# A spectral filter and a dense layer over one LayerNorm, on one core: W1 loaded in rows, the first two tiles worked with the contraction outermost, two more tiles turned by DMA

## The chip, the core and the metric

The kernel runs on one core of a Trainium2 chip. The core has five engines that run their own instruction lists: TensorE (PE: matmul, with its weight loads shown as PEld), VectorE (DVE), ScalarE (ACT), GpSimd (POOL) and SyncE (SP, which here only issues DMAs). They meet through semaphores. Data lies in DRAM, in SBUF (128 partitions) and in PSUM (eight banks of 512 f32 columns for 128 partitions, which TensorE writes). The metric is the device time of one execution in microseconds; the profile's span is the part of it that the hardware profiler shows.

## What is computed

```python
xn = _layernorm(x, axis=-1)                       # x: (1, 2048, 640) bf16
# A: spectral filter over both axes
X = rfft2(xn.astype(float32)) * (w_r + 1j * w_i)   # 2048 x 321
a = irfft2(X, s=(2048, 640)).astype(bfloat16)
# B: dense layer
h = gelu(xn @ w1 + b1)                            # w1: 640 x 1536, tanh form of gelu
b = h @ w2 + b2                                   # w2: 1536 x 640
return x + a + b
```

## The kernel before, in words

The 2,048 tokens are 16 tiles of 128; token 16p + c lies in partition p of tile c. Each tile goes through these steps:

- **x load** (`load_x`, L585): tiles 0 and 1 alone (160 KB each), the rest in pairs (320 KB).
- **LayerNorm** on VectorE: two `bn_stats` (L662) of 320 columns, one `bn_aggr` (L664), then rstd on GpSimd (L666), then the norm itself, one `tensor_scalar` of 640 columns (L684) into the tile `T`.
- **Turning.** The first layer contracts over the 640 columns, so the normed tile is transposed into `xnT`, as five blocks of 128 x 128 (the index j). Tiles 0 to 5 are turned by TensorE (L703, five transposes a tile into a PSUM tile `tps`), and copied to `xnT` by VectorE (L558) or ScalarE (L557). The tiles in `BYDMA` (L449), 6 to 15, are turned by a DMA that SP issues (L691).
- **First layer** (L735 to L753): W1 is held as five rows of 1,536 columns, one for each j. `BLOCKS` (L446) says which tiles are worked together: tile 0 alone, tile 1 alone, then pairs, then fours. For each block and each of 12 column groups fc, five matmuls over j, in two steps of three and two, fill one PSUM bank `hps`, and ScalarE puts the gelu of it into `gT` (L751). A matmul is 128 columns wide for a block of one tile, 256 for two, 512 for four.
- **Stage A** on the same normed tiles: VectorE folds a pair of tiles (L713, L717), TensorE multiplies by `gtab` (ten matmuls of 128 columns a pair), the result is copied into `XV`. The later stages of the filter (etab, mtab, the product with W at L818, ntab, getab, htab) follow from about 45 us on.
- **Second layer** (`second`, L904): from `gT` and W2, closed by the filter's last product, added to x + b2 on VectorE and stored.

W1 comes in four transfers (`W1P`, L447, `load_w1`, L592), cut by column groups: fc 0 to 2, 3 to 6, 7 to 9, 10 and 11. Each carries all five rows j, as pieces of 768, 1,024, 768 and 512 bytes, and a group fc needs the one transfer that holds its columns.

**Order.** Every operation gets a number as it is made (`K.op`), and `ORDER` (L159) writes out by hand, for each engine, the list of numbers in which it issues them; an engine never passes an instruction that waits. Waits are worked out from what each operation reads and writes. SP's list is the order of its one DMA queue. The tables `ROW_NS` and `LAG` stand in a model of time in `schedule`, which with a written order only decides which PSUM banks and buffers are taken.

SP's list begins 8 (x tile 0), 12 (x tile 1), 13, 14 (W1 pieces 0, 1), 15 (x tiles 2 and 3), 16, 17 (W1 pieces 2, 3), 19 (x 4 and 5), 18 (gtab), and so on; 165 and 167 are the turns of tiles 6 and 7, behind ten more loads.

Of the kernel before, what the change touches and what calls it, by code (L numbers as in the profile page):

```python
# [9 lines left out]
ACT = mybir.ActivationFunctionType  # L10
# [3 lines left out]
D = 640  # L14
F = 1536
# [83 lines left out]
def mm_us(n):  # L99
    return max(n / 2400.0 + 0.0027, 0.0265)  # L100
# [24 lines left out]
class Pool:  # L125
# [34 lines left out]
    "sp": """8 12 13 14 15 16 17 19 18 20 25 29 21 26 48 24 30 34 42 165 167 28 49 44 178 180 191 193 47 41 27 36  # L160
38 33 32 40 39 206 204 220 218 46 43 35 31 50 37 45 52 525 522 523 524 546 549 548 547 51 572 573 570 571 596 594
595 597 623 650 659 640 614 695 676 686 767 758 712 732 722 783 749 792 799 806""",
    "pe": """7 53 116 114 121 119 235 236 238 239 232 271 233 274 272 268 269 275 283 284 250 251 280 281 247 248 244 245 277 286 278 241
# [8 lines left out]
777 710 778 730 720 747 779 780 786 793 787 781 794 795 788 796 789 790 797 800 801 802 803 804""",  # L172
    "act": """11 9 10 117 54 122 237 240 234 273 270 276 285 252 282 249 246 279 288 243 294 255 291 261 136 264 300 330 309 297 306 131
# [3 lines left out]
578 579 651 590 593 468 615 750 759 480 687 465 474 477 599 775 784 626 471 483 662 697 735 734 769 770""",  # L177
    "dve": """0 55 56 59 57 60 61 113 118 115 120 123 124 127 125 63 64 68 65 67 69 134 126 137 128 139 140 141 145 144 75 74
# [15 lines left out]
class Ring:  # L194
# [4 lines left out]
    def issue_end(self, t, us, n):  # L199
        end = t + us  # L200
        while True:
# [770 lines left out]
```

## Time and profile before

| | us |
|---|---|
| median of 3 runs (149.04 to 149.48) | 149.30 |
| the profiled execution | 149.13 |
| its span | 147.1 |
| busy in it: VectorE | 109.9 |
| ScalarE | 85.8 |
| GpSimd | 23.0 |

Times in the profile's rows are microseconds from the span's start. A row of a timeline reads: start, length, engine, line of the kernel, operation, what it writes and reads, shapes, and how many in a row (x24); a row of several starts with the first and ends with the last, and rows can overlap, since instructions are pipelined. In brackets stands how long the engine idled before it and what it waited for. `ps` is PSUM, `T` the normed tiles, `W` in a matmul of `xnT,W` is W1. All matmuls but the transposes have one line, L546, and are told apart by their operands. TensorE's clock was granted in full in every slice of the span.

### The profile page before, as it was taken

The page shows a single profiled execution, that of the slowest core. Times are in us where ns is not written, and L with a number is a line of the kernel's source. Part 1 is how long each engine was busy: PE and PEld are TensorE (multiplying, and loading weights), DVE is VectorE, ACT ScalarE, POOL GpSimd, SP SyncE. Part 2 cuts the span into 40 slices and gives each one's busy share as a digit, 9 for nine tenths or more (in the row PEclk, how much of TensorE's full clock was granted, in tenths as well). Part 3 has the DMA queues.
Part 4 walks back from the last instruction along what each step waited for, and adds up shares of the span by engine and source line. Part 5 has one row for each costly group of instructions (what it writes and reads, how often), then busy time and mean ns, then how long its engine had stood idle before and what let it go on. Part 6 is the DMA issues. An engine that isn't in the chain of part 4 may idle for free.

```text
span 147.1 us, 4193 instructions
## 1 busy us (share of the span) xinstructions
PE 142.4 (97%) x1766; PEld 92.2 (63%) x1766; DVE 109.9 (75%) x231; ACT 85.8 (58%) x160; POOL 23.0 (16%) x38
## 2 busy tenths in 40 slices
PE   7799999999999999999999999999999999999993
PEld 7599999898465455456544555544447665656572
DVE  1888999999864458799687991893207899987883
ACT  3298898998899999934346637523935730312000
POOL 1302250402200007810000010200076300000000
PEclk9999999999999999999999999999999999999999
DMA  4999999995998974997706651952639950422324
GB/s 106 322 346 395 382 233 132 166 119 128 324 176 154 244 167 92 228 261 138 96 0 113 104 117 32 137 103 49 128 61 231 238 147 1 152 75 89 134 96 134
DMA packets 31546, 23.35 MB, mean 159 GB/s; under 512 B 19240, under 2 KB 28200, under 8 KB 31400
## 3 DMA queue, kind: packets, MB, share of 16 engines
q1 hardware_dynamic: 28992, 17.48, 51.6%
q0 software_dynamic: 2368, 5.57, 17.2%
q8 instruction: 14, 0.23, 0.6%
q10 hardware_dynamic: 168, 0.04, 0.1%
q14 instruction: 4, 0.03, 0.1%
HBM read 13.58 MB, written 2.62 MB: 110 GB/s over the span
## 4 chain that ended last, share of the span: by engine, by line
PE 94%; DMA 2%; DVE 1%; POOL 1%; issue 1%
PE ps L546 93%; DMA X<-in_A_x_dram 2%; PE ps L703 1%; POOL rstd L666 1%; DVE stats L662 1%; DVE T L684 0%; DVE W L929 0%; DVE mv L664 0%
## 5 line engine op out<-in xcount | busy, mean ns | idle before, releaser
L546 PE MATMUL ps<-xnT,W 128*128 128x256 bf16 (+2 forms) x420 | 58.7, 288 | 0.1
L546 PE MATMUL ps<-W,gT 128*128 128x512 bf16 (+2 forms) x396 | 58.5, 295 | 0.0
L546 PEld LDWEIGHTS ps<-W,gT 128*128 128x128 bf16 x396 | 30.1, 98 | 23.1 <-issue 1.5
L546 PEld LDWEIGHTS ps<-xnT,W 128*128 128x128 bf16 x420 | 34.5, 98 | 15.8 <-issue 1.9
L751 ACT ACTIVATE gT<-ps,b1col 128x256 bf16<-128x256 f32 (+2 forms) x84 | 38.4, 509 | 9.8 <-PE ps L546 9.2
L557 ACT ACTIVATE Wf<-ps 128x960 bf16<-128x960 f32 (+1 forms) x8 | 6.7, 869 | 16.9 <-PE ps L546 16.9
L662 DVE BATCH_NORM_STATS2 stats<-X 128x6 f32<-128x320 bf16 x32 | 14.2, 474 | 2.6 <-DMA X<-in_A_x_dram 2.6
L818 DVE TENSOR_TENSOR T<-Y,Wf 128x1288 bf16<-128x1288 bf16 x16 | 12.3, 826 | 1.5 <-DMA Wf<-in_A_w_i_dram 0.9
L914 POOL DMA_DIRECT2D X<-in_A_x_dram x8 | 7.1, 1091 | 38.1 <-DMA XV<-U 21.3
L666 POOL TENSOR_TENSOR rstd<-mv,mhalf 128x2 f32<-128x2 f32 (+1 forms) x10 | 7.1, 706 | 30.6 <-DVE mv L664 30.5
L557 ACT ACTIVATE Xb<-ps 128x960 bf16<-128x960 f32 (+1 forms) x8 | 8.7, 1124 | 5.0 <-PE ps L546 4.9
L914 POOL DMA_DIRECT2D xnT<-in_A_x_dram x8 | 7.1, 1249 | 23.1 <-DMA XV<-U 14.7
L557 ACT ACTIVATE XV<-ps 128x1280 bf16<-128x1280 f32 (+3 forms) x12 | 9.9, 858 | 0.9 <-PE ps L546 0.9
L557 ACT ACTIVATE U<-ps 128x512 bf16<-128x512 f32 (+1 forms) x12 | 4.6, 434 | 8.0 <-PE ps L546 7.9
L558 DVE CAST Y<-ps 128x644 bf16<-128x644 f32 x7 | 5.8, 827 | 4.2 <-PE ps L546 4.2
L717 DVE TENSOR_TENSOR T<-T 128x512 bf16<-128x512 bf16 (+1 forms) x32 | 8.8, 311 | 0.1
L920 DVE TENSOR_TENSOR X<-ps,X 128x640 f32<-128x640 f32 x8 | 6.5, 818 | 3.0 <-PE ps L546 3.0
L558 DVE CAST Wf<-ps 128x960 bf16<-128x960 f32 (+1 forms) x4 | 4.3, 1074 | 5.7 <-PE ps L546 5.7
L929 DVE TENSOR_TENSOR W<-ps,xnT 128x640 bf16<-128x640 f32 (+2 forms) x10 | 6.7, 686 | 2.2 <-PE ps L546 2.2
L684 DVE TENSOR_SCALAR T<-X,mv,rstd 128x640 bf16<-128x640 bf16 x16 | 6.8, 443 | 1.3 <-POOL rstd L666 1.1
L557 ACT ACTIVATE Y<-ps 128x644 bf16<-128x644 f32 x9 | 6.3, 706 | 2.6 <-PE ps L546 2.5
L546 PE MATMUL ps<-getab,XV 32*128 32x160 bf16 (+1 forms) x128 | 7.5, 241 | 0.0
(49 smaller groups left out, 134.2 us busy)
## 6 DMA issues: line engine op xcount, KB each, us to landing
W<-in_B_w_dram SPq DMA_DIRECT2D x6, 480.0 KB, 7.4
X<-in_A_x_dram POOLq DMA_DIRECT2D x8, 320.0 KB, 5.2
xnT<-in_A_x_dram POOLq DMA_DIRECT2D x8, 320.0 KB, 5.4
out_dram<-W SPq DMA_DIRECT2D x15, 160.0 KB, 1.8
X<-in_A_x_dram SPq DMA_DIRECT2D x7, 320.0 KB, 9.2
Wf<-in_A_w_i_dram SPq DMA_DIRECT2D x6, 160.5 KB, 4.4
Wf<-in_A_w_r_dram SPq DMA_DIRECT2D x6, 160.5 KB, 5.6
W<-in_B_w_dram SPq DMA_DIRECT2D x1, 640.0 KB, 6.3
```

The lines of the kernel that those rows point to most:

```text
L546: ins = e.matmul(o_, lhsT=lw, rhs=rh, start=st, stop=sp_, skip_group_check=True)
L557: return e.activation(dst(), src(), ACT.Copy, scale=scale)
L558: return e.tensor_copy(dst(), src())
L662: st_op[c] = K.op([("dve", 0.393)], pr, lambda e, _, c=c, h=h: e.bn_stats(stats[:, c, 6 * h:6 * h + 6], view(X, c * D + H2 * h, [[1, H2]]) ...
L666: K.op([("pool", 0.65)], 500, lambda e, _, a=a, b=b: e.tensor_tensor(out=rstd[:, a:b], in0=mv[:, a:b, 1], in1=mhalf[:, a:b], op=ALU.pow), ...
L684: o = K.op([("dve", 0.356)], pr, lambda e, _, c=c, n=n, xnv=xnv: e.tensor_scalar(out=xnv(n, 0, [[1, D]]), in0=view(X, c * D, [[1, D]]), sc ...
L717: ring_ops.append(K.op([("dve", dve_us(4 * w, 2))], pr, lambda e, _, op=op, x1v=x1v, xfv=xfv, o_=o_, o0=o0, o1=o1, w=w: e.tensor_tensor(ou ...
L751: K.op([("act", act_us(128 * nt, 1))], pr + PRIO["gelu"] + GP[bi], lambda e, _, c0=c0, nt=nt, fc=fc, hps=hps: e.activation(gT[:, fc, 128 * ...
L818: filt_ops.append(K.op([("dve", dve_us(4 * KP, 2))], pr, lambda e, _, k=k, Y=Y, TB=TB, pair=pair: e.tensor_tensor(out=view(TT, TB.slot * 8 ...
L914: xo_ops[c] = K.op([("pool", 0.9)], 51 - c / 20, lambda e, _, c=c, xov=xov: e.dma_start(xov(0, D), xv[:, c, :], accum_op=ALU.add), reads=[ ...
L920: kept_ops.append(K.op([("dve", dve_us(D))], 30, lambda e, _, kps=kps, xov=xov: e.tensor_tensor(out=xov(0, D), in0=psb(kps.slot, [[1, D]]) ...
L929: K.op([("dve", dve_us(w))], 95, lambda e, _, os_=os_, fps=fps, o0=o0, w=w, xov=xov, base=base: e.tensor_tensor(out=view(W1, OST + os_.slo ...
```

## The change

Four things are changed in the program, and the order of all engines is written anew.

1. **W1 in five transfers**, one for each row j: 128 partitions of 3,072 bytes, 384 KB each (`load_w1`). A matmul of the first layer in tiles 2 to 15 now names all five as read, one of the first block only its own row j.
2. **Tiles 0 and 1 in one block.** `BLOCKS` begins with (0, 2). In this block two column groups share one PSUM bank (256 columns each), so that six banks hold all twelve, and the operation is one pair of groups and one j. For j < `LONE` = 2 there is one operation for each of the two tiles (two matmuls of 128 columns), for j = 2 to 4 one for both (two matmuls of 256). Of one pair only the first operation (j = 0, tile 0) has to stand ahead of the others, which the lists may put in any order. The gelu works on both tiles, 256 columns.
3. **Tiles 0 and 1 turned in other parts.** Blocks j = 0, 1 are transposed together and copied by ScalarE, j = 2 to 4 together and copied by VectorE (before: 0 to 2 VectorE, 3 and 4 ScalarE). Tile 0's norm is cut in two, 256 columns and 384, and its first two transposes wait for the first only. The later blocks have buffer names of their own (`B_xnL`), so that a matmul waits for its part alone.
4. **Tiles 4 and 5 turned by DMA** (`BYDMA` from 4), issued by SP.

The numbers in the new lists: SP's 8 and 12 are x tiles 0 and 1, 13, 14, 15, 17, 18 the rows of W1, 16 x tiles 2 and 3, 20, 21, 22 the pairs from 4, 6 and 8, 19 gtab, 26, 30, 27 the pairs from 10, 14 and 12, 25 the first part of W2, 154 and 152 the turns of tiles 5 and 4, 165 and 167 those of 6 and 7. On TensorE 7 is the warm-up, 54 turns b1, 116 and 118 turn tile 0 (j = 0, 1 and j = 2 to 4), 121 and 123 tile 1, 137 and 140 tiles 2 and 3; 232 to 285 are the first block, nine numbers for each pair of groups (for the first: 232 and 233 are j = 0 of tiles 0 and 1, 234 and 235 j = 1, 236, 237, 238 j = 2, 3, 4, and 239 and 240 the two gelus); 286 to 321 are tiles 2 and 3, three numbers for each group, 322 to 357 tiles 4 and 5; 131 and 132, 148 and 149, 161 and 162 are stage A of the first three pairs. On VectorE 56 and 57 are tile 0's statistics and 58 its aggregate, 60 to 62 the same for tile 1, 114 and 115 the two parts of tile 0's norm, 120 tile 1's, 119 and 124 copies of turned blocks, 125 to 130 the first pair's folds, 64 and 65 tile 2's statistics, 151 and 153 the norms of tiles 4 and 5.

```diff
@@ -157,33 +157,33 @@
 ORDER = {
-    "sp": """8 12 13 14 15 16 17 19 18 20 25 29 21 26 48 24 30 34 42 165 167 28 49 44 178 180 191 193 47 41 27 36
...
-    "pe": """7 53 116 114 121 119 235 236 238 239 232 271 233 274 272 268 269 275 283 284 250 251 280 281 247 248 244 245 277 286 278 241
...
-    "dve": """0 55 56 59 57 60 61 113 118 115 120 123 124 127 125 63 64 68 65 67 69 134 126 137 128 139 140 141 145 144 75 74
...
+    "sp": """8 12 13 14 16 15 17 18 20 22 21 19 26 30 27 25 154 152 165 167 45 31 48 29 34 47 191 178 193 180 43 44
+32 49 33 38 50 204 218 206 220 41 28 51 37 39 40 42 46 36 35 505 507 506 529 504 531 528 530 52 552 553 555 554
...
+    "pe": """7 54 116 118 250 277 268 121 123 241 232 259 251 242 278 269 260 233 270 262 279 252 280 235 243 234 281 244 245 261 263 271
+236 254 253 273 272 137 264 274 140 265 237 238 256 255 316 317 319 295 246 282 296 247 289 320 292 290 293 310 131 132 304 305
+307 301 311 302 149 148 283 286 308 298 313 299 287 314 161 162 325 322 326 323 331 343 332 344 337 338 352 353 388 361 349 389
...
+    "act": """11 10 9 55 117 122 138 276 266 267 239 258 275 257 240 318 248 297 249 291 321 294 133 135 134 306 303 312 150 309 300 288
...
+    "dve": """0 56 57 58 61 60 62 114 115 120 119 126 125 124 130 64 65 68 66 69 128 70 127 136 129 139 142 143 141 144 147 72
+73 75 76 74 77 146 145 80 151 153 79 83 82 81 84 86 156 164 155 166 157 158 159 160 97 93 94 89 90 169 91 96
...
+    "pool": """1 3 2 5 59 63 4 67 71 78 85 99 24 92 106 6 23 113 588 624 650 660 614 686 706 696 634 723 598 670 758 742
...
@@ -205,9 +205,9 @@
-ROW_NS = {256: 26, 384: 22, 512: 27, 640: 33, 642: 70, 768: 37, 1024: 47, 1280: 56, 1600: 68, 2560: 103, 4096: 160, 10272: 750, "acc": 152}
+ROW_NS = {256: 26, 384: 22, 512: 27, 640: 33, 642: 70, 768: 37, 1024: 47, 1280: 56, 1600: 68, 2560: 103, 3072: 122, 4096: 160, 10272: 750, "acc": 152}
 TAIL = 0.9
-LAG = ((1.6, 1.1), (3.9, 2.8), (16.0, 1.6), (60.0, 0.0))
+LAG = ((1.1, 0.35), (1.6, 1.3), (4.6, 2.8), (16.0, 1.6), (60.0, 0.0))
...
@@ -443,10 +443,10 @@
         block.tensor(run("pe"))
 
 
-BLOCKS = [(0, 1), (1, 1), (2, 2), (4, 2), (6, 2), (8, 4), (12, 4)]
-W1P = [(0, 3), (3, 7), (7, 10), (10, 12)]
+BLOCKS = [(0, 2), (2, 2), (4, 2), (6, 2), (8, 4), (12, 4)]
+LONE = 2
 GROUPS = [(0, 2), (2, 3), (5, 3), (8, 3), (11, 3), (14, 2)]
-BYDMA = tuple(range(6, 16))
+BYDMA = tuple(range(4, 16))
 ANY = [(0, 8)]
 ZONE = {"hps": [(4, 8)], "bps": [(0, 4)], "cps": [(0, 4)], "dps": [(0, 4)],
         "eps": [(0, 4)], "fin": [(4, 8), (0, 4)], "fps": [(4, 8)], "tps": ANY, "aps": ANY}
@@ -457,7 +457,7 @@
 KEEP = (0, 2, 3, 5, 6, 8, 9, 10, 11)
 HOME = tuple(sorted((KEEP + tuple(c for c in range(16) if c not in KEEP))[-8:], key=lambda c: (c not in KEEP, c)))
 FOLD = (1.3, 1.8, -3.2, 66.3, 45.3, 69.8, 50.8, 17.3)
-GP = (-81.0, 42.0, 4.0, 72.0, -32.0, 6.0, -9.0)
+GP = (-81.0, 4.0, 72.0, -32.0, 6.0, -9.0)
 G1 = 1
 WAVE = (0, 3, 0, 0, 2, 0, 0, 4, 0, 2, 0, 2, 4, 2, 2, 3)
 WARM = (38, 0)
@@ -576,7 +576,7 @@
 
         B_id, B_b1, B_b2b = Buf("ident"), Buf("b1t"), Buf("b2")
         B_x = [Buf(f"x{g}") for g in range(16)]
-        B_w1s = [Buf(f"w1_{j}") for j in range(len(W1P))]
+        B_w1s = [Buf(f"w1_{j}") for j in range(5)]
         B_g, B_e, B_m, B_n, B_ge, B_h, B_w2 = [Buf(x) for x in ("g", "e", "m", "n", "i", "h", "w2")]
         B_w = [Buf(f"W{ri}") for ri in range(2)]
 
@@ -590,8 +590,7 @@
             return o
 
         def load_w1(j, q="sp"):
-            a, b = W1P[j]
-            load(view(W1, 128 * a, [[F, 5], [1, 128 * (b - a)]]), w1v[:, :, 128 * a:128 * b], B_w1s[j], (40, 256 * (b - a)), q=q)
+            load(view(W1, F * j, [[1, F]]), w1v[:, j, :], B_w1s[j], (8, 2 * F), q=q)
         load_x(0, 1)
         K.op([("act", 1.3)], 420, lambda e, _: e.preload_act_table(ACT.Gelu_apprx_tanh), writes=[Buf("table")])
         load(ident[:], const["I"], B_id, (8, 256), q="act", prio=410)
@@ -599,9 +598,10 @@
         load_x(1, 1)
         load_w1(0)
         load_w1(1)
+        load_w1(2)
         load_x(2, 2)
-        load_w1(2)
         load_w1(3)
+        load_w1(4)
         load(gtab[:], const["G"], B_g, (8, 4096), issue=0.5)
         load_x(4, 2)
         load_x(6, 2)
@@ -649,6 +649,7 @@
         K.op([("act", 0.2)], 200, lambda e, _: e.activation(b1col[:], psb(B_b1ps.slot, [[1, NFC]]), ACT.Copy), reads=[B_b1ps], writes=[B_b1c])
 
         B_xnT = [Buf(f"xnT{c}") for c in range(16)]
+        B_xnL = [[B_xnT[c]] * 2 + [Buf(f"xnT{c}")] * 3 for c in range(2)]
         B_xa = [Buf(f"xa{c}") for c in range(8)]
         norm_ops, ring_ops, a_ops, TD = [], [], [], {}
         B_rs = [Buf(f"rstd{c}") for c in range(16)]
@@ -681,10 +682,13 @@
                 c = 2 * pair + n
                 pr = 100 - c / 2
                 B_xn = Buf(f"xn_{c}")
-                o = K.op([("dve", 0.356)], pr, lambda e, _, c=c, n=n, xnv=xnv: e.tensor_scalar(
-                    out=xnv(n, 0, [[1, D]]), in0=view(X, c * D, [[1, D]]), scalar1=mv[:, c, 0:1], scalar2=rstd[:, c:c + 1], op0=ALU.subtract, op1=ALU.mult),
-                    reads=[B_x[c], B_rs[c]], writes=[xn, B_xn])
-                norm_ops.append(o)
+                cuts = (0, 256, D) if not c else (0, D)
+                B_xs = [Buf(f"xn_{c}") for _ in cuts[2:]] + [B_xn]
+                for d0, d1, bx in zip(cuts, cuts[1:], B_xs):
+                    o = K.op([("dve", 0.066 + (d1 - d0) / 1980.0)], pr, lambda e, _, c=c, n=n, xnv=xnv, d0=d0, d1=d1: e.tensor_scalar(
+                        out=xnv(n, d0, [[1, d1 - d0]]), in0=view(X, c * D + d0, [[1, d1 - d0]]), scalar1=mv[:, c, 0:1], scalar2=rstd[:, c:c + 1], op0=ALU.subtract, op1=ALU.mult),
+                        reads=[B_x[c], B_rs[c]], writes=[xn, bx])
+                    norm_ops.append(o)
                 if not c:
                     st_op[1].gate += [o] * G1
                 if c in BYDMA:
@@ -694,7 +698,7 @@
                     if c % 2:
                         turned[(c - 5) // 2].append(TD[c])
                     continue
-                for j0, j1, engs in ((0, 3, ["dve"]), (3, 5, ["act"])) if c < 2 else ((0, 5, ["dve", "act"]),):
+                for j0, j1, engs in ((0, 2, ["act"]), (2, 5, ["dve"])) if c < 2 else ((0, 5, ["dve", "act"]),):
                     nj = j1 - j0
                     tps = Buf(f"tps{c}", psum, 1, ZONE["tps"])
 
@@ -702,12 +706,14 @@
                         for j in range(j0, j1):
                             ins = e.transpose(psb(tps.slot, [[1, 512]]).bitcast(BF)[:, 128 * j:128 * j + 128], xnv(n, 128 * j, [[1, 128]]), ident[:])
                         return ins
-                    tp = K.op([("pe", nj * mm_us(128))], pr, xt, reads=[B_xn, xn, B_id], writes=[tps], alts=[[("128", nj * mm_us(128))]])
+                    tp = K.op([("pe", nj * mm_us(128))], pr, xt, reads=[B_xs[0] if j0 == 0 else B_xn, xn, B_id], writes=[tps], alts=[[("128", nj * mm_us(128))]])
+                    if not c + j0:
+                        tp.deps.remove(norm_ops[1])
                     us = {"dve": 0.06 + 0.07 * nj, "act": act_us(128 * nj)}
                     o = K.op([(e, us[e]) for e in engs], pr,
                          copy(lambda c=c, j0=j0, j1=j1: xnT[:, c, j0:j1, :],
                               lambda tps=tps, j0=j0, j1=j1: psb(tps.slot, [[1, 512]]).bitcast(BF)[:, 128 * j0:128 * j1].rearrange("p (j t) -> p j t", j=j1 - j0)),
-                         reads=[tps], writes=[B_xnT[c]])
+                         reads=[tps], writes=[B_xnL[c][j0] if c < 2 else B_xnT[c]])
             pr = 100 - pair - FOLD[pair]
             for k, op in enumerate((ALU.add, ALU.subtract)):
                 K.op([("dve", dve_us(640, 2))], pr, lambda e, _, k=k, op=op, xnv=xnv, x1v=x1v: e.tensor_tensor(
@@ -735,21 +741,31 @@
         l1_ops, l1_of = [], {}
         for bi, (c0, nt) in enumerate(BLOCKS):
             for fc in range(NFC):
-                hps = Buf(f"hps{c0}_{fc}", psum, 1, ZONE["hps"])
                 bg = Buf(f"gT{c0}_{fc}")
                 for c in range(c0, c0 + nt):
                     B_gT[c, fc] = bg
                 pr = PRIO["hps"] - bi - fc / 20
-                w = [j for j, (a, b) in enumerate(W1P) if a <= fc < b][0]
-                part_ = []
-                for js in ((0, 1, 2), (3, 4)):
-                    part_ = [pe([("128", len(js) * mm_us(128 * nt))], pr + 0.01 * len(part_), lambda c0=c0, nt=nt, fc=fc, hps=hps, js=js: [
-                        (psb(hps.slot, [[1, 128 * nt]]), view(W1, F * j + 128 * fc, [[1, 128]]), xnT[:, c0:c0 + nt, j, :], j == 0, j == 4) for j in js],
-                        reads=[B_w1s[w]] + B_xnT[c0:c0 + nt], writes=[hps], gate=part_)]
-                    l1_ops += part_
-                    l1_of.setdefault(bi, []).extend(part_)
-                K.op([("act", act_us(128 * nt, 1))], pr + PRIO["gelu"] + GP[bi], lambda e, _, c0=c0, nt=nt, fc=fc, hps=hps: e.activation(
-                    gT[:, fc, 128 * c0:128 * (c0 + nt)], psb(hps.slot, [[1, 128 * nt]]), ACT.Gelu_apprx_tanh, bias=b1col[:, fc:fc + 1], scale=1.0),
+                if bi:
+                    hps, at, part_ = Buf(f"hps{c0}_{fc}", psum, 1, ZONE["hps"]), 0, []
+                    for js in ((0, 1, 2), (3, 4)):
+                        part_ = [pe([("128", len(js) * mm_us(128 * nt))], pr + 0.01 * len(part_), lambda c0=c0, nt=nt, fc=fc, hps=hps, js=js: [
+                            (psb(hps.slot, [[1, 128 * nt]]), view(W1, F * j + 128 * fc, [[1, 128]]), xnT[:, c0:c0 + nt, j, :], j == 0, j == 4) for j in js],
+                            reads=B_w1s + B_xnT[c0:c0 + nt], writes=[hps], gate=part_)]
+                        l1_ops += part_
+                        l1_of.setdefault(bi, []).extend(part_)
+                else:
+                    at = 256 * (fc % 2)
+                    if not at:
+                        hps, part_ = Buf(f"hps0_{fc}", psum, 1, ANY), []
+                        for j in range(5):
+                            for t0, t1 in ((0, 1), (1, 2)) if j < LONE else ((0, 2),):
+                                part_.append(pe([("128", 2 * mm_us(128 * (t1 - t0)))], pr + 8 - j - 2 * t0, lambda fc=fc, hps=hps, j=j, t0=t0, t1=t1: [
+                                    (psb(hps.slot, [[1, 128 * (t1 - t0)]], 256 * h + 128 * t0), view(W1, F * j + 128 * (fc + h), [[1, 128]]), xnT[:, t0:t1, j, :], j == t0 == h == 0, j == 4) for h in range(2)],
+                                    reads=[B_w1s[j]] + [B_xnL[t][j] for t in range(t0, t1)], writes=[hps], gate=part_[:1]))
+                        l1_ops += part_
+                        l1_of.setdefault(bi, []).extend(part_)
+                K.op([("act", act_us(128 * nt, 1))], pr + PRIO["gelu"] + GP[bi], lambda e, _, c0=c0, nt=nt, fc=fc, hps=hps, at=at: e.activation(
+                    gT[:, fc, 128 * c0:128 * (c0 + nt)], psb(hps.slot, [[1, 128 * nt]], at), ACT.Gelu_apprx_tanh, bias=b1col[:, fc:fc + 1], scale=1.0),
                     reads=[hps, B_b1c], writes=[bg])
 
         def width(slot, n, lhs, tab):
@@ -886,7 +902,7 @@
                         return xnT[:].rearrange("p c j t -> p (c j t)").bitcast(F32)[:, D * ki + o0:D * ki + o0 + w]
                 else:
                     ki = [b for b in range(16) if b not in HOME].index(c)
-                    free = norm_ops[:2 * ki + 2]
+                    free = norm_ops[:2 * ki + 3]
 
                     def xov(o0, w, ki=ki):
                         return X[:].bitcast(F32)[:, D * ki + o0:D * ki + o0 + w]
```

More of the change, by code (lines that the diff above doesn't have):

```diff
@@ L159 @@
 ORDER = {
[L160 to L163 removed]
[8 rows of a table removed]
[L172 to L173 removed]
[3 rows of a table removed]
[L177 to L178 removed]
[5 rows of a table removed]
[L184 to L186 removed]
+    "sp": """8 12 13 14 16 15 17 18 20 22 21 19 26 30 27 25 154 152 165 167 45 31 48 29 34 47 191 178 193 180 43 44
+32 49 33 38 50 204 218 206 220 41 28 51 37 39 40 42 46 36 35 505 507 506 529 504 531 528 530 52 552 553 555 554
+53 578 577 579 576 605 596 622 641 668 632 658 677 740 731 694 749 714 765 704 774 781 788""",
+    "pe": """7 54 116 118 250 277 268 121 123 241 232 259 251 242 278 269 260 233 270 262 279 252 280 235 243 234 281 244 245 261 263 271
[8 rows of a table added]
+712 769 763 770 771 702 776 777 772 778 779 782 783 784 785 786""",
+    "act": """11 10 9 55 117 122 138 276 266 267 239 258 275 257 240 318 248 297 249 291 321 294 133 135 134 306 303 312 150 309 300 288
[3 rows of a table added]
+453 581 447 757 607 643 644 766 680 716 717 752""",
+    "dve": """0 56 57 58 61 60 62 114 115 120 119 126 125 124 130 64 65 68 66 69 128 70 127 136 129 139 142 143 141 144 147 72
[5 rows of a table added]
+648 679 647 621 631 681 676 640 682 684 683 718 667 719 657 720 721 751 739 730 748 753 693 754 755 756 713 764 703 773 780 787""",
+    "pool": """1 3 2 5 59 63 4 67 71 78 85 99 24 92 106 6 23 113 588 624 650 660 614 686 706 696 634 723 598 670 758 742
+767 733""",
 }
```

3 lines of the change are left out of this document (removed), and 29 rows, old and new, of the table ORDER.

## The prediction, made before the changed kernel was run

> **What bounds the kernel now.** I read the page first: busy shares, slices, and the chain that ended last.
>
> ```profile
> span 147.1 us, 4193 instructions
> PE 142.4 (97%) x1766; PEld 92.2 (63%) x1766; DVE 109.9 (75%) x231; ACT 85.8 (58%) x160; POOL 23.0 (16%) x38
> ...
> PE   7799999999999999999999999999999999999993
> ...
> GB/s 106 322 346 395 382 233 132 166 119 128 324 176 154 244 167 92 228 261 138 96 0 113 104 117 32 137 103 49 128 61 231 238 147 1 152 75 89 134 96 134
> ...
> PE 94%; DMA 2%; DVE 1%; POOL 1%; issue 1%
> ```
>
> TensorE is full from the second slice to the last. The same chain in order of time gives the few places where it is not:
>
> ```profile
> 0.74 2.33 DMA X<-in_A_x_dram
> ...
> 3.10 0.92 DVE stats L662 x3
> 4.02 0.38 issue
> 4.39 0.22 DVE mv L664
> ...
> 4.68 0.57 POOL rstd L666
> ...
> 5.29 0.57 POOL rstd L666
> ...
> 5.88 0.46 DVE T L684
> ...
> 6.39 0.50 PE ps L703 x5
> 6.89 3.92 PE ps L546 x68
> 10.82 0.10 issue
> ...
> 19.30 0.28 PE ps L703 x5
> ...
> 20.18 0.28 PE ps L703 x5
> 20.46 124.10 PE ps L546 x1471
> ```
>
> From 6.39 us everything is TensorE work except 0.10 us at 10.82. So a change gains by less TensorE work or an earlier start, and loses by any new TensorE wait. The sum is made against the profiled execution's 149.13 us, whose span is 147.1; it lies 0.17 below the median of the three runs, 149.30, to which I add the result.
>
> **The change, part by part.** *Turns of tiles 4 and 5.* The two x5 rows at 19.30 and 20.18 are their ten TensorE transposes: 2 × 0.28 = **0.56 us off the path**. Their two ScalarE copies go too; ScalarE is not on the chain, so they count nothing.
>
> *Tiles 0 and 1 in one block.* Before, 120 matmuls of 128 columns; the chain's 68 took 3.92 us, 57.6 ns each, 6.91 us in all. After, with LONE = 2, two of the five contraction steps stay 128 wide (48 matmuls, 2.76 us) and three are 256 wide (36).
>
> ```profile
> 15.95 0.72 PE L546 MATMUL ps<-gtab,T 128*128 128x128 bf16 x10
> 16.51 2.78 PE L546 MATMUL ps<-xnT,W 128*128 128x256 bf16 x24
> 19.13 0.44 PE L703 MATMUL ps<-ident,T 128*128 128x128 bf16 x5
> ```
>
> From start to start, 24 of 256 columns took 2.62 us, 109 ns each, and ten of stage A's took 56 ns each. 36 × 109 ns = 3.92, so the block is 6.69 us: **0.22 us less**. It cannot be much better: a 128-column matmul costs little more than half a 256-column one. The 0.10 us at 10.82 is the wait for the third W1 piece (it lands at 10.73, below), and goes with the pieces: **0.10**.
>
> *The start.* The rows of before:
>
> ```profile
> 5.29 0.45 DVE L684 TENSOR_SCALAR T<-X,mv,rstd 128x640 bf16<-128x640 bf16 x1
> ...
> 5.79 1.10 PE L703 MATMUL ps<-ident,T 128*128 128x128 bf16 x10 [0.92 <-DVE T L684]
> 6.73 5.58 PE L546 MATMUL ps<-xnT,W 128*128 128x128 bf16 x90
> ...
> 6.11 0.38 ACT L557 ACTIVATE xnT<-ps 128x256 bf16<-128x256 bf16 x1 [3.43 <-PE ps L703]
> ```
>
> In the new VectorE order tile 0's aggregate no longer stands behind tile 1's statistics (the 0.38 of issue at 4.02 falls to about 0.1), but tile 1's own statistics and aggregate now stand ahead of the first norm, which so begins near 5.25 against 5.29. It does 256 columns first: 0.45 × 256/640 is some 0.2 us. Two transposes start near 5.52 (before 5.79), their ScalarE copy ends near 6.1, and the first W1 matmul waits for whichever is later, the copy or W1's first row. Landing times of before:
>
> ```profile
> 1.66 1.00 SPq L541 DMA_DIRECT2D W<-in_B_w_dram  x2
> 2.70 0.59 SPq L541 DMA_DIRECT2D X<-in_A_x_dram  x1
> 3.33 1.78 SPq L541 DMA_DIRECT2D W<-in_B_w_dram  x2
> ...
> W<-in_B_w_dram SPq DMA_DIRECT2D x1, 480.0 KB, 4.8
> ...
> W<-in_B_w_dram SPq DMA_DIRECT2D x1, 640.0 KB, 6.3
> ...
> X<-in_A_x_dram SPq DMA_DIRECT2D x1, 320.0 KB, 6.6
> ...
> W<-in_B_w_dram SPq DMA_DIRECT2D x1, 480.0 KB, 7.4
> ```
>
> Issue plus landing: 800 KB of the queue (two x tiles of 160, the first piece) are in at 6.46, 1,440 at 8.46, 1,760 at 9.30, 2,240 at 10.73. W1's first row is complete at 704 KB, by the 320 KB/us of the second piece at 6.16. So the first W1 matmul runs near 6.2 with five transposes behind it; before it ran at 6.73 with ten. Less the other five (0.28) and 0.07 in which it waits for tile 1's copy, that is **0.2 us earlier**. Bounds: nothing if the first row still lands at 6.46, 0.3 if it costs no wait.
>
> *W1's later rows.* They are complete at 1,088, 1,792, 2,176 and 2,560 KB (tiles 2 and 3 go ahead of the third row in the queue). At the slow end, the 336 KB/us of 9.30 to 10.73: 7.3, 9.4, 10.6, 11.7. At the fast end, the 381 KB/us of the x piece (320 KB between 8.46 and 9.30): 7.2, 9.0, 10.0, 11.0. The new TensorE list asks for step 1 after 12 pairs of step 0 and tile 1's transposes (near 7.9), for step 2 eight pairs later (8.85), for step 3 near 10.4, for step 4 near 11.3. So the third row is late by 0.15 to 0.55 us; once that is waited out the rest are about in time. W1's rows of 3,072 bytes are nearest to the x piece's of 2,560, so I take **0.2 us lost**. The Trainium skill ("DMA: Bandwidth & Descriptors", Specifications) puts line rate at 512 bytes a transfer and up; by it longer rows would bring nothing and the slow end would hold, 0.55 lost. The piece of 2,560-byte rows landed faster than the W1 pieces, against that.
>
> *The two added turns.* They are issued on SP behind both norms, and before the turns of tiles 6 and 7.
>
> ```profile
> 8.12 0.76 DVE L717 TENSOR_TENSOR T<-T 128x512 bf16<-128x512 bf16 x2
> 9.30 1.28 DVE L662 BATCH_NORM_STATS2 stats<-X 128x6 f32<-128x320 bf16 x3 [0.42 <-DMA X<-in_A_x_dram]
> 13.07 0.49 DVE L558 COPY xnT<-ps 128x640 bf16<-128x640 bf16 x1 [0.51 <-PE ps L703]
> 18.27 0.80 DVE L684 TENSOR_SCALAR T<-X,mv,rstd 128x640 bf16<-128x640 bf16 x2
> ...
> DMA to landing us min/median/max: 2.6/3.7/4.8
> ...
> W<-in_B_w_dram SPq DMA_DIRECT2D x1, 480.0 KB, 11.6
> ...
> 10.42 1.36 SPq L541 DMA_DIRECT2D W<-in_B_w_dram  x2
> ```
>
> From tile 2's statistics (9.30) to the norms of tiles 4 and 5 (18.27) were 8.97 us. The new order has two statistics fewer in between (0.4 each), the two 512-wide folds of pair 0 more (0.76), and should lose the 0.51 of waiting: 8.4. Tile 2's statistics start near 8.2, when x lands and VectorE is through tile 1. So the norms run from 16.6 to 17.4, one turn is issued then and the other 1.3 us on at 18.7, and by the ten turns' landing (2.6, median 3.7, 4.8) the second is in at 21.3, **22.4** or 23.5. TensorE asks for it after 6.69 + 15 transposes (0.84) + 60 matmuls of tiles 2 and 3 (6.54) + 30 of stage A (1.68) = 15.75 us from 6.2, with 0.27 of waits: 22.2. I take the median: **0.2 us lost**, bounds 0 and 1.3. The Trainium skill ("VectorE: DVE Perf Modes", The three transpose paths) gives 390 ns a block on TensorE and 1,309 by DMA and prefers TensorE where PSUM will do; ten blocks at that would be 13 us, the second turn in at 30.5, the sum near 157. Here a turn of five blocks never took over 4.8 us, and TensorE's blocks cost 56 ns.
>
> *At nothing.* VectorE does one norm as two (a fixed part of some 0.1 us in a chain that then idles for the rstd of tile 1). ScalarE's first gelus come near 11.9 instead of 7.2, but 24 runs of 128 columns become 12 of 256; with four PSUM banks of room it stays ahead of TensorE (rival below). SP's second-layer loads queued behind the turns are wanted only when the second layer begins, after 55 us. After 20.46 TensorE has one unbroken piece, the same matmuls in another order with as many switches between full and 32-row tiles: nothing to gain there, and only a new wait to lose. The end (0.33 of VectorE, then the last store) keeps its shape.
>
> Sum: −0.56 − 0.22 − 0.10 − 0.20 + 0.20 + 0.20 = −0.68. **149.30 − 0.68 = 148.6 us.**
>
> **Rivals.** *Given back at the front.* The third W1 row is 0.55 late, or ScalarE, which must now do 22 gelus of 256 columns and five copies between 11.9 and 22, gets behind the four banks. For it: TensorE's list asks within 0.15 us of my landing. Against: ScalarE's work there is about 10.9 us (gelus near 0.36 each), which leaves it 0.8 behind TensorE where four banks allow 2.2. With 0.55 for the row and no start gained: −0.88 + 0.55 + 0.2 = −0.1: 149.2, no change to be seen.
>
> *The turns come late (the other side).* Turns share SP's queue with the loads. Before, a second-layer piece issued at 10.42 landed at 22.0. In the new list such a piece stands right ahead of the two turns; if the queue drains no earlier, they land one after the other 1.3 us apart behind it, at 24.6, and TensorE stands 2.4 us at tiles 4 and 5: 149.30 − 0.88 + 2.4 = **150.8**. Against: W1 takes less of the queue, one mirrored W load is no longer ahead, and the GpSimd loads of W have been moved later. It decides once the second turn lands later than 23.1, where the stall eats all gained; from 23.5 on it is slower by over 0.3%.
>
> *Quicker still.* Nothing is late: −1.08, 148.2.
>
> **How the numbers follow.** Forecast 0.48, given back 0.19, turns late 0.27, quicker 0.06. The forecast's own range is 148.2 to 149.0; the range for all, 147.9 to 150.4, runs from a no-wait result with 0.3 us to spare to most of the late turns, and leaves out some 0.05 below and 0.12 above. A measurement here tells 0.3% (0.45 us) from no change: faster than 148.85 are the forecast but for a twelfth of it, the quicker case, and a fifth of the giving back, 0.55; slower than 149.75 the late turns but for a little, and some of the giving back, 0.27; 0.18 in between.
>
> **What would show it.** Ten matmuls fewer under L703's transposes (x20), 84 in place of 120 in the first block, the first W1 matmul near 6.2, and in the chain either no DMA of W, or a wait of some 0.2 us for it near 9. A TensorE wait near 22 for a DMA into xnT prices the turns: under 0.3 the forecast stands, over 1.0 it is wrong. Any wait of TensorE after 25 us, or a busy time of TensorE that does not fall by some 0.8 us, would make the working wrong as well.

## The result, and the profile after

The changed kernel takes **148.62 us** (median of 20 runs, 148.23 to 151.6) against 149.33 us for the kernel before (20 runs, 148.85 to 150.06): ratio **0.9965**, 95% interval 0.9948 to 0.9982. The forecast was 148.6. The profiled execution took 148.36 us with a span of 146.3, against 149.13 and 147.1.

The lines of the page that answer to those of before:

```profile
span 146.3 us, 4090 instructions
...
PE 142.4 (97%) x1720; PEld 91.2 (62%) x1720; DVE 109.2 (75%) x230; ACT 82.1 (56%) x148; POOL 22.8 (16%) x38
...
PE   7999999999999999999999999999999999999992
...
PE 94%; DMA 2%; DVE 2%; issue 0%; ACT 0%
```

TensorE's busy time is 142.4 us as before, which by the prediction's last paragraph would speak against it. It misleads: the 38 warm-up matmuls start at 0.99 in both and last 4.23 us instead of 3.77, in time in which TensorE idled before, and tile 0's transposes are slower too. Windows of TensorE, first of the changed kernel, then of the one before (window, length, busy time):

```profile
6.35:146.30 139.95, 137.35 (x1676) 1.00 0.70 159
...
6.39:147.10 140.71, 138.05 (x1722) 1.00 0.70 157
```

Behind the point where its stream begins TensorE is busy 0.70 us less, and ahead of it 0.69 us more. The chain in order of time shows where:

```profile
5.47 0.41 PE ps L707 x2
...
5.91 0.39 ACT xnT L557
...
6.35 0.51 PE ps L546 x6
6.86 0.28 PE ps L707 x5
7.13 4.12 PE ps L546 x56
...
12.25 131.46 PE ps L546 x1557
143.72 0.02 issue
143.74 0.33 DVE W L945
```

Five transposes lie behind the point where the chain turns to TensorE for good, in both kernels: at 6.39 before, at 6.35 now. So **0.04 us** came from the start. From there to the last matmul it was 138.17 us (to 144.56) and is 137.37 (to 143.72): **0.80 us** came from TensorE's stream. The two x5 rows near 20 us and the 0.10 of issue at 10.82 are gone, and after 12.25 the chain is one unbroken piece of TensorE. In the prediction's own terms the start is 0.10 earlier: the first W1 matmul runs at 6.35 instead of 6.73, and 0.28 of that are the five transposes that now come after it.

The idle times of these views are counted from the modelled end of a matmul. The trace also has the start of every single matmul, and from start to start a wait is some 0.16 us longer than a row says; a shorter one isn't shown at all. So in the kernel before TensorE stood 0.26 us at 10.92, not 0.10, and 0.13 us each at 8.53, for W1's second piece (in at 8.46), and at 13.66, for the VectorE copy that begins at 13.07.

Two transfers had been forecast late. Their rows (timeline of SP, issue to landing, timelines of TensorE and of ScalarE):

```profile
3.09 0.44 SPq L541 DMA_DIRECT2D W<-in_B_w_dram  x1
W<-in_B_w_dram SPq DMA_DIRECT2D x1, 384.0 KB, 5.9
...
6.97 4.29 PE L546 MATMUL ps<-xnT,W 128*128 128x128 bf16 x56
11.10 0.44 PE L707 MATMUL ps<-ident,T 128*128 128x128 bf16 x5
...
7.00 0.38 ACT L557 ACTIVATE xnT<-ps 128x256 bf16<-128x256 bf16 x1 [0.71 <-PE ps L707]
...
16.79 5.36 SPq L695 DMA_TRANSPOSE xnT<-T  x4
xnT<-T SPq DMA_TRANSPOSE x1, 2.9
xnT<-T SPq DMA_TRANSPOSE x1, 2.7
...
22.29 5.40 PE L546 MATMUL ps<-xnT,W 128*128 128x256 bf16 x48
```

W1's third row lands at 8.99. TensorE's 34 narrow matmuls from 6.97 start 56 ns apart, with one wait of 0.14 us, at 7.44, for tile 1's ScalarE copy (7.00 to 7.38). So it asks for the row at 9.01, goes on at 9.12 and loses 0.11. The whole stretch of 42 narrow and 14 wide matmuls takes 4.13 us (to 11.10) where 42 × 56.1 + 14 × 108.7 ns (measured below) make 3.88: the 0.25 are these two waits. The turns of tiles 5 and 4 are issued at 16.79 and 18.15, land 2.9 and 2.7 us later, at 19.7 and 20.85, and TensorE asks at 22.29. They cost nothing, with 1.4 us to spare.

### The profile page after: what moved, and what is told of

The parts are those of the page before. It is cut to its first block, busy times and chain, and to the rows that moved or that the text cites. A ratio compares the mean times of both kernels' runs of the same rounds, so it can differ in the third digit from the quotient of the medians.

```text
span 146.3 us, 4090 instructions
## 1 busy us (share of the span) xinstructions
PE 142.4 (97%) x1720; PEld 91.2 (62%) x1720; DVE 109.2 (75%) x230; ACT 82.1 (56%) x148; POOL 22.8 (16%) x38
## 4 chain that ended last, share of the span: by engine, by line
PE 94%; DMA 2%; DVE 2%; issue 0%; ACT 0%
PE ps L546 93%; DMA X<-in_A_x_dram 2%; DVE stats L663 1%; PE ps L707 1%; DVE mv L665 0%; ACT xnT L557 0%; DVE W L945 0%; DVE T L688 0%
## 5 line engine op out<-in xcount | busy, mean ns | idle before, releaser
L546 PE MATMUL ps<-xnT,W 128*128 128x256 bf16 (+2 forms) x384 | 58.0, 300 | 0.2 <-ACT xnT L557 0.2
L546 PE MATMUL ps<-W,gT 128*128 128x512 bf16 (+3 forms) x396 | 57.9, 295 | 0.0
L546 PEld LDWEIGHTS ps<-xnT,W 128*128 128x128 bf16 x384 | 33.3, 98 | 16.2 <-issue 2.2
L767 ACT ACTIVATE gT<-ps,b1col 128x256 bf16<-128x256 f32 (+1 forms) x72 | 35.1, 551 | 8.1 <-PE ps L546 8.1
L557 ACT ACTIVATE Xb<-ps 128x960 bf16<-128x960 f32 (+1 forms) x7 | 7.6, 1105 | 4.5 <-PE ps L546 4.4
L723 DVE TENSOR_TENSOR T<-T 128x128 bf16<-128x128 bf16 (+1 forms) x32 | 8.8, 310 | 0.1
L558 DVE CAST Wf<-ps 128x640 bf16<-128x640 f32 (+1 forms) x4 | 4.0, 988 | 5.8 <-PE ps L546 5.8
L558 DVE CAST Xb<-ps 128x960 bf16<-128x960 f32 (+1 forms) x5 | 5.8, 1169 | 3.2 <-PE ps L546 3.2
L688 DVE TENSOR_SCALAR T<-X,mv,rstd 128x640 bf16<-128x640 bf16 (+2 forms) x17 | 7.0, 429 | 0.7 <-POOL rstd L667 0.4
L546 PEld LDWEIGHTS ps<-getab,XV 32*128 32x128 bf16 (+1 forms) x128 | 6.5, 145 | 1.5 <-ACT Wf L557 0.3
```

Source lines behind the costliest of these rows:

```text
L546: ins = e.matmul(o_, lhsT=lw, rhs=rh, start=st, stop=sp_, skip_group_check=True)
L557: return e.activation(dst(), src(), ACT.Copy, scale=scale)
L558: return e.tensor_copy(dst(), src())
L688: o = K.op([("dve", 0.066 + (d1 - d0) / 1980.0)], pr, lambda e, _, c=c, n=n, xnv=xnv, d0=d0, d1=d1: e.tensor_scalar(out=xnv(n, d0, [[1, d1 ...
L723: ring_ops.append(K.op([("dve", dve_us(4 * w, 2))], pr, lambda e, _, op=op, x1v=x1v, xfv=xfv, o_=o_, o0=o0, o1=o1, w=w: e.tensor_tensor(ou ...
L767: K.op([("act", act_us(128 * nt, 1))], pr + PRIO["gelu"] + GP[bi], lambda e, _, c0=c0, nt=nt, fc=fc, hps=hps, at=at: e.activation(gT[:, fc ...
```

## The experiments

**All of the first block narrow.**

```diff
-LONE = 2
+LONE = 5
```

> The changed kernel with LONE = 5: the first block is 120 matmuls of 128 columns instead of 48 and 36 of 256; every list is otherwise the same. If TensorE's work sets the end (my reading), the block takes 120 x 57.6 ns = 6.91 us instead of 6.69 and the kernel is 0.2 us slower than the changed one: near 148.85, ratio to before near 0.997 to 0.998; the last TensorE instruction ends near 143.95 instead of 143.72. Rival (the gain comes from the new order and the transfers, not from the width): no difference, since weight loads hide under narrow matmuls and the lost time is taken from a wait that stands there anyway; the block then ends at the same time.

Measured: 149.71 us (6 runs, 148.73 to 151.55), ratio to before 1.0005 (0.9972 to 1.0037), which settles nothing: its profiled execution stood 0.34 and 0.72 us for rows of W1, the third of which landed at 10.19. But the same piece of work can be laid beside that of the changed kernel in a further run (c1 and c0 below are that kernel again; this is c0). First the narrow kernel, then c0, timelines of TensorE from the third row to the next transposes:

```profile
10.23 2.18 PE L547 MATMUL ps<-xnT,W 128*128 128x128 bf16 x36 [0.72 <-DMA W<-in_B_w_dram]
12.25 0.44 PE L708 MATMUL ps<-ident,T 128*128 128x128 bf16 x5
```

```profile
9.75 2.13 PE L546 MATMUL ps<-xnT,W 128*128 128x256 bf16 x22 [0.49 <-DMA W<-in_B_w_dram]
11.72 0.44 PE L707 MATMUL ps<-ident,T 128*128 128x128 bf16 x5
```

From start to start, 36 narrow matmuls take 2.02 us, 56.1 ns each. The same work as 8 narrow and 14 wide takes 1.97, so a wide one is (1.97 − 8 × 0.0561) / 14 = 108.7 ns. Two narrow for one wide cost 3.5 ns more, and 36 of them 0.13 us: the width is worth **0.13**, not 0.22. The 57.6 ns of the chain of before had the wait at 8.53 in it. In the time of the whole kernel this difference was not seen.

**Tiles 4 and 5 back on TensorE.**

```diff
-BYDMA = tuple(range(4, 16))
+BYDMA = tuple(range(6, 16))
 # SP: the turns of tiles 5 and 4 taken out
 # PE: transposes of tile 4 after the last group but one of tiles 2 and 3, of tile 5 after the last
 # ACT: their copies each between two gelus there
```

> The changed kernel with tiles 4 and 5 turned by TensorE again (ten transposes, two ScalarE copies between the gelus where a PSUM bank is free). Theory A (the prediction's: the ten transposes cost their 0.56 us on TensorE, the copies nothing): the kernel is 0.56 us slower than the changed one, near 149.2, and TensorE waits for nothing between 21 and 24 us. Theory B (ScalarE has no room there, since the twelve gelus of the first block now come after 12 us): the two copies of 0.7 us push the second past the moment when TensorE asks for tile 5 (22.9 us), TensorE waits 0.5 to 0.9 us for the copy, and the kernel is 1.1 to 1.4 slower, near 149.9.

Measured: **150.91 us** (4 runs), ratio 1.0111 (1.0081 to 1.014), span 148.6. Theory B. Timelines of ScalarE and TensorE:

```profile
22.11 0.72 ACT L557 ACTIVATE xnT<-ps 128x640 bf16<-128x640 bf16 x1
22.70 0.51 ACT L767 ACTIVATE gT<-ps,b1col 128x256 bf16<-128x256 f32 x1
23.05 0.74 ACT L557 ACTIVATE xnT<-ps 128x640 bf16<-128x640 bf16 x1
...
22.89 0.73 PE L546 MATMUL ps<-gtab,T 128*128 128x128 bf16 x10 [0.16 <-ACT xnT L557]
23.85 2.36 PE L546 MATMUL ps<-xnT,W 128*128 128x256 bf16 x20 [0.23 <-ACT xnT L557]
```

The second copy ends at 23.79 and TensorE starts on tiles 4 and 5 at 23.85. Without waits it would have been there at 23.09 (stage A of the second pair starts at 19.34 instead of 19.10, so 22.29 + 0.24, and 0.56 for the transposes): 0.76 us lost to ScalarE. A further 0.8 us goes in one wait for a gelu near 55 us, in an order that was not made for this kernel. So in this order the DMA turns are worth more than their 0.56; how much an order made for the other way would save was not tried.

**Two more loads ahead of the turns.**

```diff
 # SP
-... 27 25 154 152 165 167 45 31 ...
+... 27 25 31 28 154 152 165 167 45 ...
```

> The changed kernel with two more quarters of W2 (960 KB) put ahead of the turns of tiles 5 and 4 in SP's list. Theory of the prediction's rival (turns stand in the queue behind the loads): the queue's last load lands about 2.4 us later than the 19.1 us of the changed kernel, at 21.5, the turns land near 22.2 and 23.5 instead of 19.7 and 20.85, and TensorE, which asks for tiles 4 and 5 at 22.3, waits 1.0 to 1.5 us: near 149.8. Other theory (a turn takes its 2.7 to 2.9 us from issue to landing whatever is queued): they land where they did, no wait, near 148.6.

Measured: **152.44 us** (4 runs, 150.91 to 152.97), ratio 1.0191 (1.0145 to 1.0238). The profiled execution is the shortest of the four, 150.91 us at a mean granted clock of 1.000; the other three had 0.989, and no profile shows what they waited for. Timelines of SP and TensorE, and the landings of the last load ahead and of the second turn:

```profile
10.07 3.10 SPq L541 DMA_DIRECT2D W<-in_B_w_dram  x1
W<-in_B_w_dram SPq DMA_DIRECT2D x1, 480.0 KB, 12.3
...
18.86 1.27 SPq L695 DMA_TRANSPOSE xnT<-T  x1
xnT<-T SPq DMA_TRANSPOSE x1, 6.1
...
22.43 0.72 PE L546 MATMUL ps<-gtab,T 128*128 128x128 bf16 x10
25.00 2.23 PE L546 MATMUL ps<-xnT,W 128*128 128x256 bf16 x19 [1.85 <-DMA xnT<-T]
```

The last load ahead is in at 22.4, and the second turn now takes 6.1 us and lands at 24.9 instead of 20.85; TensorE stands 1.85 us. The rest of the 2.6 us of span is 0.7 for W1's third row, which landed at 9.7. Turns do stand behind the loads of their queue, as the prediction's slower rival had it.

**The narrow operations first.**

```diff
 # PE
-... 235 243 234 281 244 245 261 263 271 236 254 253 273 ...
+... 235 243 234 244 261 271 253 281 245 263 236 254 273 ...
```

> The changed kernel with the four narrow operations of step 1 (eight matmuls, 0.46 us) moved ahead of the first wide one of step 2 on TensorE, so that the third row of W1 (landed at 9.0) is asked for at 9.35 instead of 8.9. If TensorE stands some 0.15 us for that row in the changed kernel, it is 0.1 to 0.15 us faster, near 148.5, and the stretch from the second transposes to tile 2's is 3.98 us instead of 4.13. If the 0.18 us by which that stretch is longer than its matmuls has another cause, no difference.

Measured: 149.48 us (6 runs, 148.93 to 149.86), ratio 1.0007 (0.9983 to 1.0031): a miss. The stretch did get shorter (7.08 to 11.11, 4.03 us), but in this execution the third row landed at 8.69, before the old order would have asked for it (9.1), so that says nothing of the edit. And the profile shows a wait that the first one does not have. Timelines of SP and TensorE, and the landing of the last of the turns of tiles 8 to 11:

```profile
31.57 1.28 SPq L695 DMA_TRANSPOSE xnT<-T  x1
xnT<-T SPq DMA_TRANSPOSE x1, 4.5
...
32.48 2.58 PE L546 MATMUL ps<-xnT,W 128*128 128x256 bf16 x22
36.13 1.46 PE L546 MATMUL ps<-xnT,W 128*128 128x512 bf16 x6 [1.07 <-ACT X L912]
```

TensorE stops before the block of tiles 8 to 11. The row blames a copy on ScalarE, but such a copy releases no matmul; the turn lands at 31.57 + 4.5 = 36.07, and TensorE goes on at 36.13. In the first profile of the changed kernel the same turn was issued at 30.84 and landed at 34.24, TensorE asked near 34.9.

**The changed kernel again.**

> The changed kernel itself, beside the next two on the same chip. If landing times alone make its spread (its twenty runs went from 148.23 to 151.6, six of them at 149.47 or more), it repeats: most runs at 148.3 to 148.9, some 1.0 to 1.6 us longer, and where the profiled execution is one of the long ones, TensorE waits for a row of W1 near 9 us or for the turns of tiles 8 to 11 near 35, for the time that it is longer. If the chip makes the spread, all its runs here agree with each other.

Measured: 148.92 us (12 runs, 148.1 to 150.17), ratio 0.9973 (0.9949 to 0.9997). The profiled execution happened to be the longest, 150.17 us, span 148.2, and has both waits: the 0.49 us at 9.75 shown above, and this one (SP, landing, TensorE):

```profile
32.39 1.28 SPq L695 DMA_TRANSPOSE xnT<-T  x1
xnT<-T SPq DMA_TRANSPOSE x1, 4.4
...
33.10 2.58 PE L546 MATMUL ps<-xnT,W 128*128 128x256 bf16 x22
36.92 1.46 PE L546 MATMUL ps<-xnT,W 128*128 128x512 bf16 x6 [1.25 <-ACT gT L767]
```

The turn lands at 36.79, TensorE goes on at 36.92. 0.49 + 1.25 = 1.74 of the 1.9 us by which this span is longer; from start to start the two waits are 0.66 and 1.41. The instructions and their order are the same in both profiles; only landing times differ.

**The turns of tiles 8 to 11 ahead of two mirrored loads, twice.**

```diff
 # SP
-... 165 167 45 31 48 29 34 47 191 178 193 180 43 ...
+... 165 167 31 48 29 34 191 178 193 180 45 47 43 ...
```

> The changed kernel with two mirrored loads of W (160 KB each, in short rows) moved from ahead of the turns of tiles 8 to 11 to behind them in SP's list. In the changed kernel's profile the last of these turns lands at 34.24 and TensorE asks for tiles 8 to 11 at 34.9; in the run with the narrow operations first it landed at 36.07 and TensorE stood 1.07 us. Theory A (that wait makes the long runs): the last turn lands at 33.5 or before, no wait near 35, and the long runs become fewer: median 148.3 to 148.6. Theory B (the long runs come from W1's rows near 9 us): the same spread as the changed kernel beside it.

> The changed kernel a third time, as the measure for the next: median 148.5 to 148.9, a quarter to a third of its runs at 149.3 or more.

> The two mirrored loads behind the turns of tiles 8 to 11 once more. If the late turn of tiles 8 to 11 makes most long runs, it has again fewer of them than the changed kernel beside it (2 of 12 at 149.3 or more against 2 to 4 of 12) and a median 0.2 to 0.4 us lower; if the long runs come from W1's rows and elsewhere, the two agree within 0.1 us.

Measured: first 148.56 us (12 runs, to 149.81; ratio 0.9964, 0.9941 to 0.9987) beside 148.92 of the changed kernel, then 148.73 (12 runs, to 149.37; 0.9953, 0.9926 to 0.998) beside 148.38 (12 runs, to 150.16; 0.9955, 0.992 to 0.9989). The landing does what was expected (SP, landing, TensorE):

```profile
30.40 1.28 SPq L695 DMA_TRANSPOSE xnT<-T  x1
xnT<-T SPq DMA_TRANSPOSE x1, 2.7
...
32.59 3.87 PE L546 MATMUL ps<-xnT,W 128*128 128x256 bf16 x28
```

It is in at 33.1, and TensorE runs through (28 matmuls without a break, the last six of them of tiles 8 to 11). But the medians differ by −0.36 and +0.35: no gain that can be told. Over all runs the changed kernel has 5 of 44 at 149.9 or more and this one none of 24, which would fit the late turn; but the next kernel, which has this edit too, has three of 12. That the late turn makes the long runs is not shown. The second profile still stood 0.8 us for W1's third row.

**Both edits together.**

> The edit of the run before (mirrored loads behind the turns of tiles 8 to 11) with the four narrow operations ahead of the first wide one, which asks for W1's third row 0.46 us later. If both waits are what the long runs are made of: median 148.2 to 148.4, no run over 149.2. If neither is, the changed kernel's spread.

Measured: 148.72 us (12 runs, 148.21 to 153.93), ratio 0.9978 (0.9949 to 1.0007); four runs at 149.5 or more, where none over 149.2 was expected, and no profile shows their cause. A miss: asking 0.46 us later for the third row was no gain.

**W1 in rows alone, in the kernel before.**

```diff
-W1P = [(0, 3), (3, 7), (7, 10), (10, 12)]
...
+            load(view(W1, F * j, [[1, F]]), w1v[:, j, :], B_w1s[j], (8, 2 * F), q=q)
...
-                        reads=[B_w1s[w]] + B_xnT[c0:c0 + nt], writes=[hps], gate=part_)]
+                        reads=B_w1s + B_xnT[c0:c0 + nt], writes=[hps], gate=part_)]
```

> The kernel before with W1 in five rows and nothing else: tiles 0 and 1 apart, all five contraction steps of a column group together, turns as before. Each group now needs all five rows, the last of which lands near 11.0 (4.04 + 6.9 in the changed kernel), so TensorE's first W1 matmul moves from 6.73 to about 11.0 and, as TensorE has no idle time later to take it back, the kernel gets 4.2 us slower: near 153.4. If the later stages can take back part (VectorE and the loads would then be ahead), it is under 152.5.

Measured: **155.05 us** (one run), span 153.0. Timeline and windows of TensorE:

```profile
11.09 7.12 PE L546 MATMUL ps<-xnT,W 128*128 128x128 bf16 x90 [4.32 <-DMA W<-in_B_w_dram]
...
6.70:11.09 4.39, 0.07 (x3) 0.69 1.03 408
11.09:15.00 3.91, 3.91 (x38) 0.50 1.03 403
15.00:18.20 3.20, 3.20 (x58) 0.97 1.07 376
```

(The fourth column of a window is the granted clock.) The wait is the 4.3 us expected; the span is 5.9 longer. Behind the wait TensorE ran at a clock of 0.50 until 15 us: the 90 matmuls take 6.95 us to the next transposes where they took 5.41 before, 1.5 us more. Nothing was taken back later. By themselves the rows cost 5.9 us here; only with the contraction outermost did they not.

**The start, with tile 0's norm waited for as a whole.**

```diff
-                    if not c + j0:
-                        tp.deps.remove(norm_ops[1])
```

> The changed kernel, but tile 0's first two transposes wait for both parts of its norm, as if it were not cut. The second part ends about 0.25 us after the first, so the transposes start near 5.7 instead of 5.47, the ScalarE copy begins near 6.15 instead of 5.91 and the first W1 matmul comes near 6.6 instead of 6.35, if the copy sets it: 0.2 us more of span, unless a wait at 9 us for W1's third row gives it back (then the matmuls of step 2 begin where they did, and the span stays). Rival: the first W1 row sets it (it lands between 6.2 and 6.5), no difference at all.

Measured: **159.0 us** (one run). Neither theory had that. The waits of TensorE in this kernel:

```profile
PE ps L546 <- ACT gT L765: 7.4, 13, 1.0
```

Thirteen waits for gelus, 7.4 us in all. The longer wait had moved the planner's times, and with them the PSUM banks: 48 tiles have another bank than in the changed kernel. One of them is the pair of column groups 10 and 11 of the first block, whose last gelu comes late (at 40.71 in the changed kernel and 50.38 here, not 35 as the next expectation has it): it came to lie in bank 5, one of the four that the first layer of the later tiles uses, where the changed kernel has it in bank 0. So the same edit with the banks held:

```diff
         K.schedule()
+        tp0.deps.append(norm_ops[1])   # tp0: tile 0's first transposes
         K.sync()
```

> The same wait as in the run at 159.0 us (tile 0's first two transposes wait for both parts of its norm), added after the PSUM banks have been given out, so that every tile lies in the bank in which it lies in the changed kernel; there the bank of column groups 10 and 11 of the first block, held until 35 us, was bank 0, in the run at 159.0 it was bank 5, one of the four that the first layer of the other tiles uses. Theory A (the bank made the 159.0): no waits of TensorE for gelus between 15 and 50 us, first W1 matmul near 6.48, time near 148.7. Theory B (the later start did, by pushing ScalarE behind): again near 159.

Measured: 148.91 us (9 runs, 148.35 to 154.12), ratio 0.9986 (0.9943 to 1.0028). Theory A holds for the banks together: all of them are held here, and the waits for gelus are gone. That the one pair made them, which keeps one of four banks until the last of those waits ends (50.91), is likely but not shown by itself. Its timeline of TensorE:

```profile
6.60 0.51 PE L546 MATMUL ps<-xnT,W 128*128 128x128 bf16 x6 [0.31 <-ACT xnT L557]
...
9.68 2.13 PE L546 MATMUL ps<-xnT,W 128*128 128x256 bf16 x22 [0.25 <-DMA W<-in_B_w_dram]
```

The first W1 matmul comes 0.25 us later than in the changed kernel, but step 2 starts at 9.68, when the third row lands (9.6). In c0 it started at 9.75 with the first matmul at 6.42. Where the row is late, the earlier start is worth nothing.

## Why the prediction was right

*The bound.* Right: TensorE's stream sets the end from 6.4 us on, and its waits add up to the differences between spans (1.74 of 1.9 in c0, 1.85 + 0.7 of 2.6 with the loads ahead).

*Ten transposes, 0.56.* Right in size: TensorE's stream was shortened by 0.80, and 0.56 is its largest part. That the ScalarE copies "count nothing" is not so in the new order: put back, they held TensorE 0.76 us.

*The width, 0.22.* The right mechanism, mis-sized: 0.13, from rows in which narrow matmuls run without gaps.

*The wait of before, 0.10.* Mis-sized: 0.26 at 10.92 from start to start, and the waits of 0.13 at 8.53 and at 13.66 went too. "Everything is TensorE work except 0.10 us" took the chain's pieces for work without gaps.

*The start, 0.20.* Wrong in the first profile: 0.10 earlier, less 0.14 for tile 1's copy, where 0.07 had been allowed. The step that failed is "their ScalarE copy ends near 6.1"; it ended at 6.29. I took the copy to begin some 0.2 us after the first two transposes; it began 0.44 after (5.47 to 5.91). The row of before has 0.32 (5.79 to 6.11), and it was in the prediction. The other 0.12 is TensorE's speed: in this execution the warm-up matmuls started 107 ns apart to their end, and the two transposes still took 0.41 us in the chain, while in the profile of before the matmuls had gone over to 56 ns near 4.1 us. In five of the twelve profiled executions with this front the copy began 0.43 or 0.44 after the transposes, in the other seven 0.32 or 0.33. In c1, one of the seven, it ended at 6.13 and the first W1 matmul ran at 6.19, as predicted. In two executions that matmul waited for W1's first row instead, to 6.46 and 6.50.

*W1's third row, 0.20 lost.* 0.11 in the first profile, but that was one of the better landings. Over the same twelve it came 5.6 to 7.1 us after its issue, at 8.7 to 10.2, the median at 9.44, against the asking at 9.01: typically some 0.5 lost. The median is the slow end of the prediction (9.4 by the 336 KB/us of W1's pieces). The argument from the x piece's faster landing rested on one execution. The Trainium skill ("DMA: Bandwidth & Descriptors", Specifications) has line rate from 512 bytes on, by which longer rows bring nothing; the median here fits that better than my choice.

*The turns, 0.20 lost.* Nothing lost. The norms came at 15.96 instead of 16.6, and on a queue that had nearly drained (the core's DMA moved 369 GB/s between 16 and 17 us and 109 in the next; the last load ahead is in at 19.1) a turn took 2.7 to 2.9, not the median 3.7 that stood for a fuller one. In the profile of the narrow kernel, where the turns were issued 1.2 us later, the second took about 4.3 us, to 23.6, and TensorE stood some 0.1 to 0.2 us at 23.5. The slower rival's mechanism was right: with two more loads ahead it became real at 1.85 us.

*The sum.* From start to start: −0.56 for the transposes, −0.13 for the width, −0.52 for the three waits of before, −0.10 for the start, +0.14 for tile 1's copy, +0.11 for the third row and +0.15 for small waits near 36, 39 and 51 us make −0.91. The last matmul starts 0.84 earlier (143.47 instead of 144.31), so 0.07 is not accounted for; the profiled times differ by 0.77. That the median came out at −0.71 against the predicted −0.68 is in part luck: the waits of before gave 0.42 more and the turns 0.20 more than forecast, the start with tile 1's copy 0.24 less, and the third row's landing alone moves by more than the whole gain from one execution to the next.

*What was missed.* "Any wait of TensorE after 25 us" was to count against the working, and in some executions there is one: the turns of tiles 8 to 11, with 0.6 us to spare in the first profile and 1.07 and 1.25 late in two others. The prediction looked for a new wait at tiles 4 and 5 only, though the same loads stand ahead of both. With the third row it makes 1.74 us in the longest run of c0; not all long runs are explained.

## What to carry to other kernels

Where one engine is full to the end, count its instructions out and you have the gain; then look, for each transfer that it asks for, at the spare time between landing and asking, in more than one execution: here 0.6 us of spare in one profile was a wait of 1.25 in another. A transfer's landing belongs to its queue: with two more loads ahead the same turn took 6.1 us instead of 2.7, and work that is taken off an engine and given to a queue stands behind the loads there. Before an edit is judged, see that it moved nothing else: 0.25 us of wait put 48 tiles into other PSUM banks and cost 10 us.

## What had not been expected of the hardware

The same list of transfers landed its sixth one between 5.6 and 7.1 us after issue from one execution to the next. TensorE's warm-up matmuls started 107 ns apart and went over to 56 ns at a time that moved from near 3.7 us (c1) to after 5.2 (the first profile), while the view of the granted clock says 1.00 all the time. And a TensorE wait of 4.32 us was followed by 3.9 us at a granted clock of 0.50, which made it cost 5.9; waits of up to 1.85 us left the clock at 1.00 in the profiled executions. The Trainium skill ("TensorE: Matmul & The Clock Gate", Why this matters for your kernels) tells to leave no gap over about 3 us between matmuls, and the trace agrees: 4.32 us halved the clock and 1.85 did not.
